# Top-k attention and a rational FFN on one core: planner lengths set anew, weight signs and weight roundings given to GpSimd, steps in another order

## The chip, the cores and the metric

The kernel runs on one core of a Trainium2 chip. The metric is the device time of one execution in microseconds, the median over runs. A core has five instruction queues that run side by side: TensorE (PE), VectorE (DVE), ScalarE (ACT), GpSimd (POOL) and SyncE (SP, which only issues transfers here). Each queue works strictly in its own order, and engines wait for each other through semaphores.

## The reference

Attention over 8 batches of 8 heads, 576 positions, head size 64, where every row keeps only its 32 largest scores; its output, as 4608 tokens of 512 features, goes through a feed-forward layer whose activation is a quotient of polynomials.

```python
scores = (q @ k.T) / sqrt(64)
kth    = 32nd largest of each row
attn   = softmax(where(scores >= kth, scores, -1e9))
x      = (attn @ v)                       # reshaped to 4608 x 512
h      = x @ w_in                         # 512 x 2048
P      = a[0] + a[1]*h + a[2]*h**2 + a[3]*h**3
Q      = 1 + |b[0]|*|h| + |b[1]|*h**2
out    = (P / (Q + 1e-6)) @ w_out         # 2048 x 512
```

The two weight matrices reach the kernel as 64-bit floats.

## The kernel before, in words

The program is written by a planner. `add(engine, length, emit, after, key, ...)` enters a step with the engine or the engines that may run it, an assumed length, what it must follow and a priority. `Plan.run` then plays all steps forward by these lengths: whenever an engine is free, `choose` takes the ready step with the smallest key and calls its `emit`, so the order of the play is the order of the program on each engine. Nothing of this is decided on the chip: lengths and keys move instructions, and the chip's own durations then decide what waits. A table, `KEY`, holds the priorities, which engines a step may use (the first named has it at once, another only after a delay from `ALT`), and how strongly TensorE is kept at one kind of matmul (`STF`, `STR`).

**Weights.** 32 blocks of 128x512 (`w0` to `w31`; 16 of `w_in`, 16 of `w_out`) are rebuilt from 64-bit words in `weight_block`: a load (SP), `sign` (L388 on GpSimd or L391 on ScalarE), `ends` (L394, ScalarE), `merge` (L399, VectorE), `size` (L404, ScalarE, an absolute value), `join` (L412, GpSimd, sign times size), then `high_part`, a rounding to TensorE's short format (`affine`, L283 on ScalarE or L285 on GpSimd) into `win_h` or `wout`, `low_part` (L429, GpSimd, the remainder), and `put` (SP), which stores the remainder to be fetched again later.

**Attention.** A unit is 128 rows of one pair of heads (named batch_pair_tile). Per head: scores `s` on TensorE (L695 in plain 32-bit for batch 0, L699 in the short format later, L690 for tail rows), a copy `sb` on ScalarE (L706), the top-32 search on VectorE (L710 to L764), a bias `st` (L291 and L842 on GpSimd around `junk` L833 and `z` L838 on ScalarE), the exponential `e` (L803, ScalarE), masked products `pr` (L807, VectorE), transposes `trp` (L962, TensorE), copies `p` (L294, ScalarE), and `av` (L986), probabilities times values.

**FFN ("moe").** 18 chunks of 256 tokens, each in 8 groups: `ph` (L1165, 24 matmuls: high times high, low times high, high times low parts), the polynomials on ScalarE and GpSimd, `gg` (a rounding, L283 or L285, and its remainder L1234 on GpSimd), and `po` (L1318, 12 matmuls). `m0_0_3` is group 3 of chunk 0 of batch 0.

Attention of one batch runs beside the FFN of the batch before it; in batch 0 it runs beside the rebuilding of the weights.

Of the kernel before, what the change touches and what calls it, by code (L numbers as in the profile page):

```python
# [36 lines left out]
class Plan:  # L37
# [54 lines left out]
    def run(self):  # L92
# [12 lines left out]
        while left:  # L105
            assert events, "the plan is stuck"
            now = max(now, heapq.heappop(events)[0])
            while ends and ends[0][0] <= now + 1e-9:
                for h in heapq.heappop(ends)[2].give:
                    h.users -= 1  # L110
                    if h.users == 0:
                        self.ring[h.tag][h.slot] = now
                        self.left[h.tag] += 1
            again = True
            while again:
                again = False
                for e in engines:
                    if free[e] > now + 1e-9:
                        continue
                    q = soon[e]  # L120
                    while q and q[0][0] <= now + 1e-9:
                        s = heapq.heappop(q)[2]
                        heapq.heappush(ready[e], (s.key, s.n, s))
                    s = self.choose(e, ready[e], q, now)
                    if s is None:
                        continue
                    for h in s.take:
                        self.grab(h)
# [12 lines left out]
                    heapq.heappush(events, (s.end, s.n))
                    if s.give:
                        back = s.end + (2.2 if e == "SP" else self.BACK)
                        heapq.heappush(ends, (back, s.n, s))
                        heapq.heappush(events, (back, s.n))
                    for d in s.next:
                        lag = max(self.LAG[e][a] + (a != e) * KEY['SLACK'].get(a, 0.0) for a in d.alts)
                        d.ready = max(d.ready, s.end + lag + d.later)
                        d.wait -= 1
                        if not d.wait:  # L150
                            for i, a in enumerate(d.alts):
                                at = d.ready + (KEY['ALT'][a] * d.alt if i else 0.0)
                                heapq.heappush(soon[a], (at, d.n, d))
                                heapq.heappush(events, (at, d.n))
                            heapq.heappush(events, (d.ready, d.n))
        return now

    def choose(self, e, ready, soon, now):
        kept, got = [], None
        closed = set()  # L160
        stay = KEY['STF'] if self.kind == "f" else KEY['STR']
        items = sorted(ready, key=lambda i: (i[0] - stay * self.stays(e, i[2]), i[1]))
        ready.clear()
        for n, item in enumerate(items):
            s = item[2]
# [14 lines left out]
        s = got[2]  # L180
# [10 lines left out]
def tile_topk_attention__then__rational_ffn(  # L191
# [28 lines left out]
    QL = QF // 2  # L220
# [5 lines left out]
    HW = KEY['HW']  # L226
# [10 lines left out]
    def add(*args, **kwargs):  # L237
        return plan.add(*args, **kwargs)
# [434 lines left out]
    def add_tile(t):  # L673
# [255 lines left out]
    def add_values(u):  # L929
# [221 lines left out]
    def add_group(x, o, g, key, split, xs, oholds):  # L1151
# [392 lines left out]
```

## Time and profile before

| | us |
|---|---|
| median of 3 runs (lowest, highest) | 1460.62 (1460.04, 1462.09) |
| the profiled execution, its own time | 1459.78 |
| span of its trace | 1458.0 |
| TensorE busy in the span | 1382.9 (95%) |
| ScalarE / VectorE / GpSimd busy | 1305.3 / 1301.1 / 1126.6 |

The profiled execution took 1.78 us more than its span; that share lies around the first and last instruction. A stretch of time is named by its microseconds from the start of the span ("0 to 205"). Matmuls overlap in TensorE, so their pace is read from the distance of their starts, not from one duration.

### The profile page before, as it was taken

What the parts mean: (1) busy time and instruction counts of PE and PEld (TensorE: products, weight loads), DVE (VectorE), ACT (ScalarE), POOL (GpSimd) and SP (SyncE); (2) the same over time, 40 slices, a digit from 0 to 9 for tenths busy, and PEclk for the clock granted to TensorE, in tenths of its full rate; (3) what the DMA queues carried; (4) which work ended last, traced back from release to release, by engine and by line L of the source; (5) the groups of instructions that cost most, each with busy time, mean ns of one, the idle gap of its engine ahead of it and who ended that gap; (6) DMA issues with size and microseconds to landing.
All of it is one profiled execution on the core that took longest, in us unless ns stands there. A gap on an engine that the chain in (4) does not pass through costs nothing.

```text
span 1458.0 us, 32829 instructions
## 1 busy us (share of the span) xinstructions
PE 1382.9 (95%) x9569; PEld 1155.3 (79%) x9569; DVE 1301.1 (89%) x5826; ACT 1305.3 (90%) x2925; POOL 1126.6 (77%) x1761
## 2 busy tenths in 40 slices
PE   4667899999999999999999999999999999999997
PEld 2435678888888878888888888888888888888995
DVE  7999989999999999999999999999999999996000
ACT  7888899999999998999899999999999999999673
POOL 5786687687867887779688877778777976876995
PEclk9777899999999999999999999999999999999999
DMA  7656766668666867577666777678667766664564
GB/s 249 232 175 210 218 215 201 184 190 248 192 211 183 245 193 226 162 223 225 210 211 202 221 224 213 186 212 224 212 182 215 228 185 216 181 189 145 173 210 118
DMA packets 162687, 296.67 MB, mean 203 GB/s; under 512 B 22976, under 2 KB 73152, under 8 KB 162496
## 3 DMA queue, kind: packets, MB, share of 16 engines
q1 hardware_dynamic: 162496, 294.47, 66.1%
q8 instruction: 78, 1.28, 0.4%
q14 instruction: 113, 0.93, 0.2%
HBM read 229.64 MB, written 18.87 MB: 170 GB/s over the span
## 4 chain that ended last, share of the span: by engine, by line
PE 79%; ACT 7%; DVE 7%; POOL 3%; DMA 2%; issue 1%; SPq 0%; ACTq 0%; POOLq 0%
PE ph_m L1165 22%; PE po_m L1318 21%; PE av L986 9%; PE trp L962 8%; PE s L699 8%; PE ph_t L1165 3%; PE po_t L1318 3%; PE s L690 2%; DVE pr L807 1%; ACT e L803 1%; PE s L695 1%; DVE m L748 1%; PE av L999 1%; ACT sb L706 1%; ACT p L294 1%
## 5 line engine op out<-in xcount | busy, mean ns | idle before, releaser
L1318 PE MATMUL po_m<-wout,gg_m 128*128 128x512 f32 x1024 | 336.9, 410 | 1.7 <-ACT ob_m L294 1.1
L1165 PE MATMUL ph_m<-xh_m,win_h 128*128 128x256 f32 x1024 | 301.7, 295 | 2.9 <-ACT w_w L404 1.7
L1165 PE MATMUL ph_m<-xh_m,wi_m 128*128 128x256 f32 x1024 | 288.4, 282 | 1.0 <-DMA wi_m<-win_l 1.0
L1165 PE MATMUL ph_m<-xl_m,win_h 128*128 128x256 f32 x1024 | 289.1, 282 | 0.0
L748 DVE MAX8 m<-all 128x8 f32<-128x144 f32 (+1 forms) x864 | 266.2, 308 | 4.7
L807 DVE SCALAR_TENSOR_TENSOR pr<-sb,m,e 128x576 f32<-128x576 f32 x288 | 232.2, 807 | 17.5 <-ACT e L803 15.5
L706 ACT COPY sb<-s 128x576 f32<-128x576 f32 x288 | 184.1, 644 | 54.3 <-PE s L699 33.2
L962 PE MATMUL trp<-ident,pr 128*128 128x128 f32 x1312 | 217.5, 282 | 12.9 <-ACT p L294 11.0
L803 ACT ACTIVATE e<-sb,st 128x576 f32<-128x576 f32 x288 | 216.4, 752 | 12.7 <-DVE hi L740 7.2
L294 ACT COPY p<-trp 128x512 f32<-128x512 f32 (+1 forms) x448 | 208.8, 481 | 10.9 <-PE trp L962 10.2
L1165 PEld LDWEIGHTS ph_m<-xh_m,win_h 128*128 128x128 f32 x1024 | 194.1, 190 | 22.4 <-issue 8.8
L1228 POOL TENSOR_TENSOR pa_m<-pa_m,hv_m 128x512 f32<-128x512 f32 x128 | 165.3, 1293 | 59.3 <-ACT hv_m L1225 58.5
L962 PEld LDWEIGHTS trp<-ident,pr 128*128 128x128 f32 x1312 | 162.8, 144 | 53.3 <-ACT p L294 18.5
L1318 PE MATMUL po_m<-wl_m,gg_m 128*128 128x512 f32 x512 | 202.3, 395 | 0.0
L1165 PEld LDWEIGHTS ph_m<-xl_m,win_h 128*128 128x128 f32 x1024 | 194.8, 190 | 2.3
L1165 PEld LDWEIGHTS ph_m<-xh_m,wi_m 128*128 128x128 f32 x1024 | 194.7, 190 | 1.6 <-DMA wi_m<-win_l 1.4
L1318 PEld LDWEIGHTS po_m<-wout,gg_m 128*128 128x128 f32 x1024 | 172.1, 189 | 28.8 <-issue 2.3
L1247 POOL TENSOR_TENSOR pa_m<-pa_m,hv_m 128x512 f32<-128x512 f32 x128 | 165.5, 1293 | 21.8 <-ACT hv_m L283 12.3
L759 DVE MATCH_REPLACE8 all<-m,all 128x144 f32<-128x144 f32 x576 | 168.7, 293 | 0.0
L1234 POOL TENSOR_TENSOR gg_m<-pa_m,gg_m 128x512 fp32r<-128x512 f32 x128 | 165.3, 1293 | 3.3 <-ACT gg_m L283 0.2
L986 PE MATMUL av<-p,vm 128*64 128x256 f32 x1280 | 160.4, 399 | 3.1 <-ACT p L294 3.1
L986 PEld LDWEIGHTS av<-p,vm 128*64 128x64 f32 x1280 | 89.8, 143 | 62.7 <-issue 10.5
(123 smaller groups left out, 3538.9 us busy)
## 6 DMA issues: line engine op xcount, KB each, us to landing
wi_m<-win_l SPq DMA_DIRECT2D x128, 512.0 KB, 4.0
wl_m<-wout_l SPq DMA_DIRECT2D x256, 256.0 KB, 3.3
vm<-in_v_dram SPq DMA_DIRECT2D x96, 320.0 KB, 3.2
q<-qx SPq DMA_DIRECT2D x224, 128.0 KB, 2.8
km<-in_qk_dram SPq DMA_DIRECT2D x32, 352.0 KB, 3.4
w_w<-in_moe_w_in_dram SPq DMA_DIRECT2D x16, 512.0 KB, 5.1
w_w<-in_moe_w_out_dram SPq DMA_DIRECT2D x16, 512.0 KB, 4.8
out_dram<-ob_m SPq DMA_DIRECT2D x64, 128.0 KB, 2.7
```

The source lines that it names most:

```text
L294: (nc.scalar.copy if plan.at == "ACT" else nc.vector.tensor_copy)(out, x)
L706: nc.scalar.copy(t.sb, t.s[:, :, 0:HF])
L748: nc.vector.max(t.m[:, o : o + 8], getattr(t, src))
L759: nc.vector.match_replace(y, t.m[:, o : o + 8], x, NEG)
L803: nc.scalar.activation(t.e, t.sb, AF.Exp, scale=SCALE, bias=t.st)
L807: nc.vector.scalar_tensor_tensor(out=t.pr, in0=t.sb, scalar=t.kth, in1=t.e, op0=ALU.is_ge, op1=ALU.mult, accum_out=u.ss[:, t.h : t.h + 1] ...
L962: nc.tensor.transpose(u.ps[i][:, c * P : (c + 1) * P], u.pr[:, x], ident)
L986: nc.tensor.matmul(pair.av[d, 0 : 2 * P], lhs, x, start=(c == 0), stop=(c == NJ))
L1165: nc.tensor.matmul(y.ph[:, f * NT : (f + 1) * NT], w, z[:, c, :], start=(c == 0 and i == 0), stop=(c == HP - 1 and i == 2),)
L1228: engine().tensor_tensor(out=y.pa, in0=y.pa, in1=y.va, op=ALU.mult)
L1247: nc.gpsimd.tensor_tensor(out=x, in0=x, in1=z, op=ALU.mult)
L1318: nc.tensor.matmul(o.po[i], z, w, start=(ff == 0 and n == 0), stop=(ff == NF - 1 and n == 2),)
```

## The change

The planner's numbers change, and with them which engine runs two kinds of weight steps. In `KEY`, 40 of 72 entries have other numbers and one, `STA`, is new; the table stands on one line in the file, and only the entries with a name or an engine in the text are shown here.

```diff
 KEY = {
...
-       'WH': ('ACT', 'POOL'),
+       'WH': ['POOL', 'ACT'],
...
-       'AV': -3.535776,
+       'AV': 4.132998,
...
-       'SB': ['ACT'],
+       'SB': ['POOL', 'ACT'],
...
-       'STF': 119.319167, 'STR': 12.516198,
+       'STA': 67.169251, 'STF': 30.907148, 'STR': 2.560445,
...
@@ class Plan
     BACK = 0.17
-    CHANGE = 0.085
+    IN, OUT = {"f": 0.0, "r": 0.0, "a": 0.143}, 0.247
@@ Plan.run
-                        if s.kind == "r" != self.kind:
-                            s.length += self.CHANGE
+                        if s.kind != self.kind:
+                            s.length += self.IN[s.kind] + (self.OUT if self.kind == "a" else 0.0)
@@ Plan.choose
-        stay = KEY['STF'] if self.kind == "f" else KEY['STR']
+        stay = KEY[{"f": 'STF', "a": 'STA'}.get(self.kind, 'STR')]
@@ lengths
-    dma = lambda n, words: max(0.52 * n, words * 4 / 260e3)
+    dma = lambda n, words: max(0.52 * n, words * 4 / 295e3)
@@ plain scores
-                    give=[kv.khold, u.pair.q.hold], crit=True, kind="f" if kv.plain else "r")
+                    give=[kv.khold, u.pair.q.hold], crit=True, kind="a" if kv.plain else "r")
@@ av
-                    take=[] if m else [avh] + ([] if u.chunk.parts or u.mixed else [u.chunk.hold]))
+                    take=[] if m else [avh] + ([] if u.chunk.parts or u.mixed else [u.chunk.hold]), kind="a")
@@ polynomials
-            e2 = add("ACT", 0.62, size, [e1], ku + 0.2, give=[mm])
+            e2 = add("ACT", act(512), size, [e1], ku + 0.2, give=[mm])
```

`WH` names the engines of the weights' rounding, `SB` those of the weights' sign. The play now gives 21 of the 32 signs and 29 of the 32 weight roundings to GpSimd; before, ScalarE had all 64. Of other roundings 9 go from GpSimd to ScalarE and 3 the other way. A sign made by GpSimd is one `tensor_scalar` with two operations over every second 32-bit word. VectorE and TensorE keep the same instructions in another order.

GpSimd at the start of the program, from its 13th row, before:

```order
L412 TENSOR_TENSOR w_w0_1_135<-w_w0_0_133,w_w0_1_135 128x512
L291 TENSOR_SCALAR st_0_0_0_166<-m_0_0_0_165 128x2
L429 TENSOR_TENSOR w_w0_0_133<-w_w0_1_135,win_h_80 128x512
L412 TENSOR_TENSOR w_w1_1_138<-w_w1_0_136,w_w1_1_138 128x512
L784 TENSOR_TENSOR fl_0_246<-all_0_0_0_158,m_0_0_0_165 128x2x3
L788 TENSOR_TENSOR fl_0_246<-m_0_0_0_165 128x2
L429 TENSOR_TENSOR w_w1_0_136<-w_w1_1_138,win_h_80 128x512
L842 TENSOR_TENSOR st_0_0_0_166<-st_0_0_0_166,z_0_0_0_209 128x2
```

and of the change:

```order
L388 TENSOR_SCALAR w_w0_1_139<-w_w0_0_137 128x512
L388 TENSOR_SCALAR w_w1_1_147<-w_w1_0_145 128x512
L388 TENSOR_SCALAR w_w2_1_162<-w_w2_0_160 128x512
L412 TENSOR_TENSOR w_w0_1_139<-w_w0_0_137,w_w0_1_139 128x512
L388 TENSOR_SCALAR w_w3_1_180<-w_w3_0_178 128x512
L291 TENSOR_SCALAR st_0_0_0_169<-m_0_0_0_168 128x2
L285 TENSOR_SCALAR win_h_80<-w_w0_1_139 128x512
L412 TENSOR_TENSOR w_w1_1_147<-w_w1_0_145,w_w1_1_147 128x512
L429 TENSOR_TENSOR w_w0_0_137<-w_w0_1_139,win_h_80 128x512
```

Signs (L388) stand ahead of the joins now, and the rounding into `win_h` (L285) stands here between join and remainder (L429); before, GpSimd had only joins and remainders of the weights.

TensorE around the first `po` (group 0 of chunk 0; `s_0_3_2_1` are the scores of batch 0, pair 3, tile 2, second head), before:

```order
L1165 MATMUL ph_m0_0_1_1820<-xh_m0_0_872,wi_m0_0_1_543 128x256
L1318 MATMUL po_m0_0_0_1965<-wout0_81,gg_m0_0_0_1798 128x512 x2
L1318 MATMUL po_m0_0_0_1965<-wl_m0_0_0_0_530,gg_m0_0_0_1798 128x512
L962 MATMUL trp0_0_2_1_1973<-ident_65,pr_0_2_1_1825 128x128 x4
L1318 MATMUL po_m0_0_1_1983<-wout0_81,gg_m0_0_0_1798 128x512 x2
L1318 MATMUL po_m0_0_1_1983<-wl_m0_0_0_0_530,gg_m0_0_0_1798 128x512
L695 MATMUL s_0_3_2_0_1997<-ka_0_2_216,q_0_2_2_1528 128x288 x2
```

and of the change:

```order
L695 MATMUL s_0_3_2_0_1934<-ka_0_2_192,q_0_2_2_1505 128x288 x2
L962 MATMUL trp0_0_2_1_1950<-ident_65,pr_0_2_1_1857 128x128 x4
L962 MATMUL trp1_0_2_1_1960<-ident_65,pr_0_2_1_1857 128x128 x4
L962 MATMUL trp2_0_2_1_1980<-ident_65,pr_0_2_1_1857 128x128
L695 MATMUL s_0_3_2_1_2005<-ka_0_2_192,q_0_2_2_1505 128x288 x2
L1318 MATMUL po_m0_0_0_2018<-wout0_81,gg_m0_0_0_1965 128x512 x2
L1318 MATMUL po_m0_0_0_2018<-wl_m0_0_0_0_472,gg_m0_0_0_1965 128x512
L1165 MATMUL ph_m0_0_1_2032<-xh_m0_0_885,win_h_80 128x256
L1165 MATMUL ph_m0_0_1_2032<-xl_m0_0_886,win_h_80 128x256
```

The first `po` stood ahead of the scores `s_0_3_2_0` and `s_0_3_2_1`; it now stands behind both. Ahead of it stood the 48 `ph` of two groups before, and stand the 24 `ph` of one now.

TensorE ahead of `av_0_3_3`, the last full block of batch 0, before:

```order
L1165 MATMUL ph_m0_0_5_2624<-xh_m0_0_872,win_h_80 128x256
L1165 MATMUL ph_m0_0_5_2624<-xl_m0_0_873,win_h_80 128x256
L1165 MATMUL ph_m0_0_5_2624<-xh_m0_0_872,wi_m0_0_5_2496 128x256
L1318 MATMUL po_m0_0_1_1983<-wout5_86,gg_m0_0_2_2461 128x512 x2
L1318 MATMUL po_m0_0_1_1983<-wl_m0_0_2_1_2035,gg_m0_0_2_2461 128x512
L962 MATMUL trp1_0_3_3_2711<-ident_65,pr_0_3_3_2583 128x128 x4
L690 MATMUL s_1_4_3_0_2722<-km_1_3_2657 128x288 x2
L699 MATMUL s_1_0_0_0_2732<-ka_1_0_1537,q_1_0_0_2090 128x288 x4
L962 MATMUL trp2_0_3_3_2743<-ident_65,pr_0_3_3_2583 128x128
L1318 MATMUL po_m0_0_0_1965<-wout6_87,gg_m0_0_3_2671 128x512 x2
L1318 MATMUL po_m0_0_0_1965<-wl_m0_0_3_0_2482,gg_m0_0_3_2671 128x512
L986 MATMUL av_0_3_3_2757<-p0_0_2_3_2537,vm_0_3_2_2166 64x256
```

and of the change:

```order
L1165 MATMUL ph_m0_0_4_2545<-xl_m0_0_886,win_h_80 128x256
L1165 MATMUL ph_m0_0_4_2545<-xh_m0_0_885,wi_m0_0_4_2381 128x256
L1318 MATMUL po_m0_0_0_2018<-wout3_84,gg_m0_0_1_2304 128x512 x2
L1318 MATMUL po_m0_0_0_2018<-wl_m0_0_1_1_639,gg_m0_0_1_2304 128x512
L962 MATMUL trp1_0_3_3_2635<-ident_65,pr_0_3_3_2510 128x128 x4
L1318 MATMUL po_m0_0_1_2098<-wout3_84,gg_m0_0_1_2304 128x512 x2
L1318 MATMUL po_m0_0_1_2098<-wl_m0_0_1_1_639,gg_m0_0_1_2304 128x512
L1318 MATMUL po_m0_0_0_2018<-wout4_85,gg_m0_0_2_2499 128x512 x2
L1318 MATMUL po_m0_0_0_2018<-wl_m0_0_2_0_2196,gg_m0_0_2_2499 128x512
L962 MATMUL trp2_0_3_3_2669<-ident_65,pr_0_3_3_2510 128x128
L690 MATMUL s_1_4_3_0_2671<-km_1_3_2598 128x288 x2
L986 MATMUL av_0_3_3_2682<-p0_0_2_3_2477,vm_0_3_2_2245 64x256
```

Before, `ph` of group 5 and `po` of group 3 stand ahead of that `av`; now it is `ph` up to group 4 and `po` up to half of group 2. Counted over the whole program ahead of it, 144 `ph` and 39 `po` became 120 `ph` and 27 `po`.

## Rows read from the trace of the kernel before

**Rows 1.** Page, busy time of the engines, and the group of `pr`.

```profile
PE 1382.9 (95%) x9569; PEld 1155.3 (79%) x9569; DVE 1301.1 (89%) x5826; ACT 1305.3 (90%) x2925; POOL 1126.6 (77%) x1761
...
L807 DVE SCALAR_TENSOR_TENSOR pr<-sb,m,e 128x576 f32<-128x576 f32 x288 | 232.2, 807 | 17.5 <-ACT e L803 15.5
```

**Rows 2.** Busy time by stretch: PE, PEld, DVE, ACT, POOL, granted clock, DMA, GB/s.

```profile
0.00:205.00 205.00, 145.89 (x659) 94.42 (x660) 185.09 (x782) 171.15 (x386) 145.37 (x260) 0.82 0.68 215
205.00:1350.00 1145.00, 1139.06 (x8305) 973.67 (x8304) 1115.55 (x5043) 1067.44 (x2430) 891.00 (x1414) 1.00 0.68 205
1350.00:1458.00 108.00, 97.94 (x610) 87.22 (x608) 0.42 (x2) 66.69 (x110) 90.20 (x89) 0.97 0.53 167
```

**Rows 3.** Waits of DVE, 0 to 225: total, times, longest us.

```profile
DVE s L724 <- ACT sb L706: 10.3, 7, 7.0
DVE pr L807 <- ACT e L803: 8.5, 13, 1.1
```

**Rows 4.** Waits of PE, 0 to 210.

```profile
PE s L695 <- DVE pr L807: 19.6, 10, 4.4
```

**Rows 5.** ScalarE, groups, 0 to 205: busy us, mean ns, idle before.

```profile
L391 ACT ACTIVATE w_w<-w_w 128x512 f32<-128x512 f32 x32 | 21.6, 675 | 1.6 <-DMA w_w<-in_moe_w_out_dram 1.0 <-DMA w_w<-in_moe_w_in_dram 0.6
...
L283 ACT ACTIVATE win_h<-w_w 128x512 fp32r<-128x512 f32 x16 | 10.1, 632 | 0.4 <-POOL w_w L412 0.3
```

**Rows 6.** Waits of POOL, 0 to 210.

```profile
POOL w_w L412 <- ACT w_w L404: 24.0, 8, 11.1
POOL w_w L429 <- ACT win_h L283: 7.7, 7, 2.2
POOL w_w L429 <- ACT wout L283: 7.7, 5, 3.1
POOL st L842 <- ACT z L838: 4.4, 5, 1.9
```

**Rows 7.** POOL, the group of biases, 0 to 205.

```profile
L842 POOL TENSOR_TENSOR st<-st,z 128x2 f32<-128x2 f32 (+1 forms) x20 | 3.9, 196 | 4.5 <-ACT z L838 4.4
```

**Rows 8.** ScalarE, timeline at 74 and 128 us: start, duration.

```profile
74.05 0.62 ACT L283 ACTIVATE wout<-w_w 128x512 fp32r<-128x512 f32 x1
128.16 0.63 ACT L283 ACTIVATE wout<-w_w 128x512 fp32r<-128x512 f32 x1
```

**Rows 9.** DVE, timeline: a wait for `e`, at 76 us.

```profile
76.06 0.81 DVE L807 SCALAR_TENSOR_TENSOR pr<-sb,m,e 128x576 f32<-128x576 f32 x1 [0.51 <-ACT e L803]
```

**Rows 10.** DVE, timeline: a wait for `e`, at 129 us.

```profile
129.65 0.82 DVE L807 SCALAR_TENSOR_TENSOR pr<-sb,m,e 128x576 f32<-128x576 f32 x1 [0.62 <-ACT e L803]
```

**Rows 11.** POOL, groups by shape over the whole span.

```profile
L1234 POOL TENSOR_TENSOR gg_m<-pa_m,gg_m 128x512 fp32r<-128x512 f32 x128 | 165.3, 1293 | 3.3 <-ACT gg_m L283 0.2
L285 POOL TENSOR_SCALAR gg_m<-pa_m 128x512 fp32r<-128x512 f32 x126 | 78.2, 621 | 5.0 <-PE po_m L1318 2.7
```

**Rows 12.** TensorE, timeline at 420 us.

```profile
420.11 0.28 PE L1165 MATMUL ph_m<-xh_m,win_h 128*128 128x256 f32 x1
420.23 0.28 PE L1165 MATMUL ph_m<-xl_m,win_h 128*128 128x256 f32 x1
```

**Rows 13.** TensorE, timeline at 1447 us, the last `po`.

```profile
1446.97 0.63 PE L1318 MATMUL po_m<-wout,gg_m 128*128 128x512 f32 x2
1447.44 0.40 PE L1318 MATMUL po_m<-wl_m,gg_m 128*128 128x512 f32 x1
```

**Rows 14.** TensorE, timeline at 216 us, `av_0_3_3`.

```profile
216.46 2.38 PE L986 MATMUL av<-p,vm 128*64 128x256 f32 x20 [0.25 <-ACT p L294]
```

**Rows 15.** DVE, timeline at 208 us, second `pr` of that pair.

```profile
207.76 0.80 DVE L807 SCALAR_TENSOR_TENSOR pr<-sb,m,e 128x576 f32<-128x576 f32 x1
```

**Rows 16.** POOL, timeline at 148 us, the first `gg`.

```profile
148.50 0.63 POOL L285 TENSOR_SCALAR gg_m<-pa_m 128x512 fp32r<-128x512 f32 x1
```

**Rows 17.** Chain that ended last, 0 to 205, shares by line.

```profile
by line: PE s L695 10.1%; PE av L986 7.2%; issue 6.5%; PE trp L962 5.3%; POOL cf L460 5.0%; ACT e L803 4.6%; PE ph_m L1165 4.2%; DVE pr L807 3.9%; ACT p L294 3.8%; ACT sb L706 3.5%; POOL w_w L429 3.3%; ACT w_w_b L394 3.3%; POOL w_w L412 3.3
```

More of the change, by code (lines that the diff above doesn't have):

```diff
@@ L19 @@
 PSUM = bass.MemoryType.PSUM
-KEY = {'OB': 16, 'K0': -0.28899, 'W0': 8.051968, 'STAY': 0.0, 'WH': ('ACT', 'POOL'), 'XH': ('POOL', 'ACT'), 'TH': 0, 'EU': 3.317342, 'SC': 0, 'HW': 256, 'Q0': ('POOL', 'ACT'), 'Q1': ('POOL',), 'SPLIT': (0, 1, 2, 3, 4, 5, 6, 7), 'XS': 1, 'P1': ('ACT', 'POOL'), 'P3': ('ACT', 'POOL'), 'RH': ('POOL', 'ACT'), 'p2': ('POOL', 'DVE'), 'p4': ('POOL',), 'ratio': ('POOL', 'DVE'), 'ratio_low': ('POOL',), 'URG': -236.940941, 'PT': 3.624573, 'AV': -3.535776, 'MOE': 250.353405, 'QT': 12.339559, 'KT': -1024.739554, 'EL': 1.0, 'LOOK': 13.192386, 'T': 5.289204, 'KL': -3.109586, 'KH': -8.857491, 'PJ': 408607.619053, 'WL': 3.813792, 'EX': 1.354535, 'EW': 32506.804284, 'ALT': {'ACT': 7.648546, 'DVE': 418.393903, 'POOL': 38.077554}, 'WG': 4.626767, 'QL': -3.100556, 'QH': -0.899155, 'PACE': 9.594453, 'B4': 0, 'RT': 1.0, 'DA': 9.729067, 'PU': (2, 2, 2, 2), 'SB': ['ACT'], 'SU': 0, 'JD': (), 'WK': -0.07211, 'PM': -5.222566, 'WI': 0, 'WO': 0, 'MS': 1.367923, 'NM': ('POOL', 'ACT'), 'WD': ('ACT',), 'LP': ('POOL',), 'FL': ('DVE',), 'VL': 548.608015, 'RI': -11.942583, 'ROOM': {'s': 2, 'mm': 2, 'o': 2, 'k': 4, 'kr': 1, 'km': 1, 'q': 2, 'qr': 1, 'v': 2, 'sb': 5, 'lo': 2, 'hi': 2, 'pr': 2, 'p0': 1, 'p1': 1, 'p2': 1, 'm': 4, 'u': 4, 'fl': 2, 'x': 2, 'xm': 1, 'xs': 1, 't': 4, 'ob': 3, 'wi': 2, 'wl': 4, 'tt': 5}, 'TN': 2, 'IL': 13.292096, 'SLACK': {'DVE': 0.0, 'PE': 0.0, 'ACT': 0.0, 'POOL': 0.0}, 'CF': 83.339795, 'LD': 0.761693, 'CL': 0.0, 'C0': 11.274467, 'ML': 1.392146, 'GL': 1.395418, 'STF': 119.319167, 'STR': 12.516198, 'SIZE': {'tt': 4096}}
@@ new lines @@
+KEY = {'OB': 16, 'K0': 13.303452, 'W0': 24.665155, 'STAY': 0.0, 'WH': ['POOL', 'ACT'], 'XH': ('POOL', 'ACT'), 'TH': 0, 'EU': -6.33561, 'SC': 0, 'HW': 256, 'Q0': ('POOL', 'ACT'), 'Q1': ('POOL',), 'SPLIT': (0, 1, 2, 3, 4, 5, 6, 7), 'XS': 1, 'P1': ('ACT', 'POOL'), 'P3': ('ACT', 'POOL'), 'RH': ('POOL', 'ACT'), 'p2': ('POOL', 'DVE'), 'p4': ('POOL',), 'ratio': ('POOL', 'DVE'), 'ratio_low': ('POOL',), 'URG': -130.582522, 'PT': -0.867947, 'AV': 4.132998, 'MOE': 65.519289, 'QT': 2.481227, 'KT': -5.785962, 'EL': 1.0, 'LOOK': 9.292689, 'T': 4.599216, 'KL': -22.168793, 'KH': 0.120246, 'PJ': 283356.121515, 'WL': 0.038413, 'EX': -8.145565, 'EW': 8862.816374, 'ALT': {'ACT': 2.797506, 'DVE': 300.280479, 'POOL': 25.426874}, 'WG': 4.452997, 'QL': -16.24214, 'QH': 11.99219, 'PACE': 10.855309, 'B4': 0, 'RT': 1.0, 'DA': 1.471092, 'PU': [2, 2, 2, 2], 'SB': ['POOL', 'ACT'], 'SU': 0, 'JD': (), 'WK': -4.152913, 'PM': -0.275068, 'WI': 0, 'WO': 0, 'MS': 1.775628, 'NM': ('POOL', 'ACT'), 'WD': ('ACT',), 'LP': ('POOL',), 'FL': ('DVE',), 'VL': 686.2294, 'RI': 8.713432, 'ROOM': {'s': 2, 'mm': 2, 'o': 2, 'k': 4, 'kr': 1, 'km': 1, 'q': 2, 'qr': 1, 'v': 2, 'sb': 5, 'lo': 2, 'hi': 2, 'pr': 2, 'p0': 1, 'p1': 1, 'p2': 1, 'm': 4, 'u': 4, 'fl': 2, 'x': 2, 'xm': 1, 'xs': 1, 't': 4, 'ob': 3, 'wi': 2, 'wl': 4, 'tt': 5}, 'TN': 2, 'IL': 15.884027, 'SLACK': {'DVE': 0.0, 'PE': 0.0, 'ACT': 0.0, 'POOL': 0.0}, 'CF': -13.594874, 'LD': 1.48874, 'CL': 2.277205, 'C0': 13.817918, 'ML': 0.0, 'GL': 3.959851, 'STA': 67.169251, 'STF': 30.907148, 'STR': 2.560445, 'SIZE': {'tt': 4096}}
```

## Prediction, made before the result

> **What bounds the kernel now.** I read the page's busy line first: TensorE is busy 95% of the span [rows 1]. A share of the whole hides where the other 5% lies, so the next view is busy time by stretch [rows 2]. From 205 to 1350 us TensorE works 1139.06 of 1145 us, so 5.9 are idle; from 1350 to the end it is idle 10.1; from 0 to 205 it is idle 59.1. Of 75.1 idle us, 59.1 lie in the start. The granted clock there is 0.82, that is between the two levels, while it is 1.00 in the middle. Only work that ends the start sooner, or puts more FFN work into it, can shorten the kernel by more than a few us.
>
> What bounds the start? VectorE is busy 185.09 of 205 us there, ScalarE 171.15, GpSimd 145.37 [rows 2]. TensorE waits for `pr` of VectorE 19.6 us before plain scores [rows 4]. So VectorE carries the start, and what delays VectorE delays all: 10.3 us for `sb`, of which one wait of 7.0 is the first score of the kernel, and 8.5 us for `e`, 13 waits [rows 3]. Without that first one, 10.3 - 7.0 + 8.5 = 11.8 us are waits on ScalarE that its queue can cause. GpSimd waits 24.0 us for ScalarE's `size`, and 7.7 + 7.7 = 15.4 for ScalarE's weight roundings [rows 6]. The chain of the start says the same: it runs through many hands, with 3.3% of 205 us each in GpSimd's remainders and joins of the weights, together 13.5 us [rows 17].
>
> **The change, part by part.**
>
> *Signs and roundings leave ScalarE.* 21 signs at 0.675 and 29 roundings at 0.632 [rows 5] are 14.2 + 18.3 = 32.5 us of ScalarE's 171.15 in the start, 19%. (Other roundings, 9 to ScalarE and 3 away, are spread over the run.) What is it worth? Such a rounding stands just ahead of the softmax chain in two cases: at 74.05 one of 0.62 us, and VectorE waits 0.51 at 76.06; at 128.16 one of 0.63, and VectorE waits 0.62 at 129.65 [rows 8 to 10]. These 1.1 us go for sure; of the other 10.7 I give 19%, the moved share of the queue, 2.0: a lower estimate of 3.1. The upper estimate takes ScalarE as a queue in which waiting goes with busy over free time: 171.15/33.85 = 5.1 before, 138.65/66.35 = 2.1 after, so 59% of 11.8 fall, 7.0. A ScalarE step that comes sooner brings forward the whole chain behind it, not only the next step, so I go nearer to the upper one: **-5.6**. The ends are 0 (the steps left on ScalarE wait for something else) and -11.8.
>
> *The same steps come to GpSimd.* A rounding costs 0.621 there [rows 11]. A sign on GpSimd is not in the trace. Its nearest row is that one-input rounding, 0.621; the dearest comparable row is a two-input step, 1.293 [rows 11]. It has one input, so I take 0.65, with both ends kept. 29 x 0.621 + 21 x 0.65 = 31.7 us; GpSimd has 205 - 145.37 = 59.6 idle in the start, so it would be at 86%. This costs nothing while the idle time covers it, and much of that idle time is waits that now vanish: the remainder (L429) no longer waits for ScalarE's rounding (15.4), and `size` comes sooner from a shorter queue (part of the 24.0). Without that cover the 31.7 us would stand in the weights' chain. The weights feed `ph`, then `gg`. The first `gg` starts at 148.50 [rows 16]; in the new order GpSimd has 18 signs, 24 roundings, 3 joins and 3 remainders more ahead of it, 18 x 0.65 + 24 x 0.621 + 6 x 1.293 = 34.4 us. Less 15.4 that is 19 us later, less all of the 24.0 it is 5 us sooner. What is queued behind each on GpSimd are 20 biases (L842) in the start [rows 7], and `e` on ScalarE, then `pr` on VectorE wait for them. Now GpSimd waits 4.4 us for ScalarE's `z` before a bias [rows 6], so it is GpSimd that is early. I cost this at 0 and keep the loss for the rivals.
>
> [...]
>
> *The new order of TensorE and VectorE.* The first `po` moves behind `s_0_3_2_1`, so the scores on which VectorE waits come first. Ahead of `av_0_3_3`, where batch 0 ends, there are now 24 `ph` and 12 `po` fewer. At full clock starts of `ph` lie 0.12 us apart [rows 12], and two `po` take 0.47 [rows 13]: 24 x 0.12 + 12 x 0.235 = 5.7 us of FFN work less done by then. It has to be done later, where TensorE is full, so it is a loss unless that `av` comes sooner. Before the change it starts at 216.46, 8.7 us after its last `pr` at 207.76 [rows 14, 15]. Of VectorE's rows, 6 fewer (some 1.4 us) stand ahead of that `pr`; with 5.7 us less in TensorE's own queue the `av` can come sooner by 1.4 to 5.7. I take the middle, 3.6, and the term is **+2.1**, with ends 0 and +4.3.
>
> *Middle and end.* From 205 to 1350 TensorE is idle only 5.9 us [rows 2]; the new kinds and stay times only reorder there, and the work is the same: 0, with ends -5.9 (all waits gone) and +6 (as many again). Behind the last `av` of batch 7 there are 24 `ph` and 15 `po` fewer than before; TensorE is full until 1447 us, so work only changes places. The last `po` begins at 1447.44 [rows 13] and copies and the last transfer follow as now: 0. The new lengths for transfers and absolute values have no cost but through the order.
>
> **Sum.** -5.6 + 2.1 = -3.5, against the profiled execution's 1459.78 (span 1458.0 and 1.78 around it) 1456.3. That execution is 0.84 under the median of the runs shown, 1460.62; against the median the sum gives **1457.1**. Its own range is 1452 to 1461. A time within 0.2% (2.9 us) of before is about what can't be told from no change.
>
> **The rivals.**
>
> *All waits for ScalarE go.* The `e` and `sb` waits vanish and the order costs nothing: 1460.6 - 11.8 = 1448.8. For it: the longest wait for `e` is 1.1 us [rows 3], so a small advance removes each whole. Against: a freed VectorE meets the next limit soon, its own 185 busy us of 205 [rows 2].
>
> *The biases eat the gain.* GpSimd at 86% delays the biases by as much as ScalarE gained: 1460.6 + 2.1 = 1462.7. For it: all joins and remainders are 1.29 us long [rows 11] and a bias of 0.196 [rows 7] sits behind one. Against: GpSimd waits 4.4 us before biases now [rows 6].
>
> *Slower: GpSimd becomes the bound of the start.* Each of 20 biases [rows 7] waits half a step of 1.29, 12.9 us, of which half is covered: 6.4. If that comes with the gain of 5.6 gone and the order's 2.1 lost, it gives 1460.6 + 2.1 + 5.3 = 1468, where 5.3 is also near 38% (31.7 us on 64 joins and remainders of 1.29, 82.6 us) of the 13.5 us that these already have in the chain [rows 17]. It decides from the point at which new waits of `e` for biases pass 3.5 us (the gain gone); from 6.4 the kernel is measurably slower.
>
> *Signs at the dear end.* At 1.293 a sign, 21 x 0.64 = 13.5 us more stand on GpSimd, 94% busy in the start; if half of it reaches the chain, 1457.1 + 6.7 = 1463.8. For it: a comparison and a subtraction over strided words, unlike a rounding. Against: one input, as the rounding at 0.621 [rows 11]. [...]
>
> **How the numbers follow.** Forecast 0.47 (0.31 of it faster by more than 0.2%, 0.14 within, 0.02 slower); all waits gone 0.12; biases eat the gain 0.13 (0.11 within, 0.02 slower); GpSimd bound 0.20; dear signs 0.08 (half within, half slower). Faster 0.43, within 0.29, slower 0.28. From 1447 to 1467 the forecast, the first and second rival, the dear signs, and the near part of the GpSimd case are held; left out are the far side of that case (0.1) and a gain beyond all waits, or a middle that changes by more than its ends (0.08).
>
> **What would show each step right or wrong.** Right: in the start ScalarE some 32 us less busy and GpSimd some 32 more; the waits of `pr` for `e` and of the fold for `sb` down from 11.8 to about 6; no wait of GpSimd's remainders on ScalarE; a sign near 0.65; waits of `e` for L842 still about 2 us; `av_0_3_3` at 211 to 215 us; TensorE's idle time from 205 to 1350 still near 6. Wrong: `e` waiting for L842 by more than 3.5 us; a sign over 0.9; VectorE's idle time in the start unchanged although ScalarE is less busy, which would say that TensorE's or VectorE's own order sets the start; or a middle whose idle time moves by several us, which would say that the new order's value lies there and not in the start.

## The result, and the profile after

The changed kernel is slower: 1476.28 us in the median of 6 runs, 1460.68 for the kernel before, a ratio (of the means of the runs, here and below) of 1.011 with a 95% interval of [1.009, 1.0131]. Of the 15.6 us between the medians the prediction had -3.5; the time lies above its range.

The busy line of the page after answers to [rows 1]; the second row is the group of `pr` in the whole span.

```profile
PE 1387.7 (94%) x9569; PEld 1161.5 (79%) x9569; DVE 1303.3 (88%) x5826; ACT 1284.5 (87%) x2880; POOL 1184.0 (80%) x1806
...
L807 DVE SCALAR_TENSOR_TENSOR pr<-sb,m,e 128x576 f32<-128x576 f32 x288 | 232.8, 808 | 34.6 <-ACT e L803 31.4
```


TensorE has the same work (1387.7 against 1382.9 us) but VectorE's `pr` waits 31.4 us for `e` where it waited 15.5. Busy time by stretch, in the columns of [rows 2], says where:

```profile
0.00:205.00 205.00, 136.68 (x567) 84.92 (x568) 172.53 (x735) 137.75 (x314) 191.36 (x293) 0.77 0.62 199
205.00:1350.00 1145.00, 1134.94 (x8262) 975.12 (x8264) 1115.76 (x5027) 1061.50 (x2415) 893.28 (x1413) 1.00 0.69 206
1350.00:1476.00 126.00, 116.04 (x745) 101.44 (x741) 14.98 (x66) 85.28 (x154) 99.33 (x102) 0.97 0.51 162
```


It is the start. There ScalarE is 33.4 us less busy (171.15 to 137.75; 32.5 were forecast), but GpSimd 46.0 us more (145.37 to 191.36; 31.7 were forecast), and VectorE and TensorE both do less (172.53 for 185.09, 136.68 for 145.89). The middle changes less: TensorE idle 10.1 us for 5.9, and a part of that still lies in batch 0, which now ends later. What filled GpSimd is in its groups from 0 to 205 us:

```profile
L388 POOL TENSOR_SCALAR w_w<-w_w 128x512 f32<-128x512 f32 x21 | 41.1, 1962 | 7.7 <-DMA w_w<-in_moe_w_in_dram 7.7
...
L285 POOL TENSOR_SCALAR wout<-w_w 128x512 fp32r<-128x512 f32 x15 | 9.4, 629 | 0.1
L285 POOL TENSOR_SCALAR win_h<-w_w 128x512 fp32r<-128x512 f32 x15 | 9.3, 623 | 0.2
```


The 30 roundings (one more than the text ahead of the prediction counts) cost 0.62 to 0.63, as the row of before had it. A sign costs 1.962 us: 41.1 us for 21, three times the 0.66 of the planner and over the dearest row that I had allowed, 1.293.

Who waits for it? First VectorE, 0 to 225 us, as in [rows 3], then ScalarE, 0 to 205:

```profile
DVE pr L807 <- ACT e L803: 21.7, 21, 3.0
DVE s L724 <- ACT sb L706: 12.3, 6, 7.0
```

```profile
ACT junk L833 <- POOL st L291: 14.2, 9, 3.6
...
ACT e L803 <- POOL st L842: 4.6, 3, 3.0
```


Waits of `pr` for `e` rose from 8.5 to 21.7. ScalarE, which was to be relieved, now waits 14.2 + 4.6 = 18.8 us for GpSimd's two small steps of the softmax bias, `st` (L291 and L842). Before it was 2.4, and GpSimd waited 4.4 us for ScalarE's `z` instead [rows 6]; ScalarE's rows of before, 0 to 205:

```profile
ACT e L803 <- POOL st L842: 2.0, 3, 1.4
ACT junk L833 <- POOL st L291: 0.4, 1, 0.4
```


GpSimd in turn waits for little after its first load (0 to 210, as in [rows 6]):

```profile
POOL w_w L388 <- DMA w_w<-in_moe_w_in_dram: 7.7, 1, 7.7
POOL st L291 <- DVE m L748: 2.5, 2, 1.7
```


The waits of 24.0, 7.7 and 7.7 us of [rows 6] are gone, as forecast, and not idle time but signs took their place. The chain of the start has moved onto GpSimd: joins, remainders, signs and roundings of weights are 53% of it, against 6.6% in [rows 17].

```profile
by line: POOL w_w L412 16.3%; POOL w_w L429 15.4%; POOL w_w L388 14.3%; issue 8.2%; POOL cf L460 8.0%; POOL win_h L285 3.7%; POOL wout L285 3.4%; DMA w_w<-in_moe_w_in_dram 2.9%; POOL kl L572 2.0%; PE av L986 2.0%; DVE pr L807 2.0%; PE s L69
```


One such case, from the timelines of GpSimd, ScalarE and VectorE around 50 us (start, duration, work, idle time before):

```profile
48.98 1.95 POOL L388 TENSOR_SCALAR w_w<-w_w 128x512 f32<-128x512 f32 x1
50.90 1.26 POOL L429 TENSOR_TENSOR w_w<-w_w,wout 128x512 fp32r<-128x512 f32 x1
52.14 0.19 POOL L291 TENSOR_SCALAR st<-m 128x2 f32<-128x2 f32 x1
```

```profile
52.36 0.32 ACT L833 ACTIVATE junk<-m,st 128x32 f32<-128x32 f32 x1 [2.35 <-POOL st L291]
...
52.68 0.73 ACT L803 ACTIVATE e<-sb,st 128x576 f32<-128x576 f32 x1
```

```profile
53.44 0.81 DVE L807 SCALAR_TENSOR_TENSOR pr<-sb,m,e 128x576 f32<-128x576 f32 x1 [2.99 <-ACT e L803]
```


A sign and a remainder stand ahead of a bias step of 0.19 us. VectorE's last step on `m` ahead of it (L748) had ended at 49.58 us, but the bias began only at 52.14, as the remainder ended (50.90 and 1.26). ScalarE idles 2.35 us for that step, its `junk` and `e` run late, and VectorE, on whose `pr` TensorE's plain scores wait 31.2 us from 0 to 210 (19.6 before [rows 4]), idles 2.99 us. By the planner's 0.66 the sign would have ended 1.3 us sooner.

Where the time goes can be summed at the end of batch 0. `av_0_3_3` started at 216.46 [rows 14]; now:

```profile
228.89 2.38 PE L986 MATMUL av<-p,vm 128*64 128x256 f32 x20
```


That is 12.4 us later, with 5.7 us less FFN work done ahead of it: 18.1 us lost there. The spans differ by 18.0 (1476.0 and 1458.0); nothing of note is lost or won behind it.

The granted clock of the start fell as well, from 0.82 to 0.77 in the mean. Its two levels show in the trace of before: 0.50 from 57 to 73 us, 1.00 from 74 to 80. One matmul of the plain scores took 632 ns from 0 to 205 in the mean, where it took 572 before. TensorE idles 68.3 us there, where it idled 59.1; how much of the 12.4 us goes through its clock is not separated by any run.

### The profile page after: what moved, and what is told of

Read it like the earlier page. It is cut to its first block, busy times and chain, and to the rows that moved or that the text cites. A ratio compares the mean times of both kernels' runs of the same rounds, so it can differ in the third digit from the quotient of the medians.

```text
span 1476.0 us, 32852 instructions
## 1 busy us (share of the span) xinstructions
PE 1387.7 (94%) x9569; PEld 1161.5 (79%) x9569; DVE 1303.3 (88%) x5826; ACT 1284.5 (87%) x2880; POOL 1184.0 (80%) x1806
## 4 chain that ended last, share of the span: by engine, by line
PE 72%; POOL 12%; DVE 6%; ACT 4%; DMA 2%; issue 2%; SPq 1%; POOLq 0%; ACTq 0%
PE ph_m L1165 22%; PE po_m L1318 20%; PE trp L962 7%; PE av L986 7%; PE s L699 7%; PE po_t L1318 3%; PE ph_t L1165 2%; POOL w_w L412 2%; POOL w_w L429 2%; POOL w_w L388 2%; PE s L690 2%; DVE m L748 1%; DVE pr L807 1%; PE av L999 1%; POOL cf L460 1%
## 5 line engine op out<-in xcount | busy, mean ns | idle before, releaser
L748 DVE MAX8 m<-all 128x8 f32<-128x144 f32 (+1 forms) x864 | 267.5, 310 | 4.3
L807 DVE SCALAR_TENSOR_TENSOR pr<-sb,m,e 128x576 f32<-128x576 f32 x288 | 232.8, 808 | 34.6 <-ACT e L803 31.4
L962 PEld LDWEIGHTS trp<-ident,pr 128*128 128x128 f32 x1312 | 163.3, 145 | 54.3 <-ACT p L294 13.6
L1247 POOL TENSOR_TENSOR pa_m<-pa_m,hv_m 128x512 f32<-128x512 f32 x128 | 165.4, 1292 | 23.7 <-ACT hv_m L283 10.8
```

Of the source, the lines that this page charges most:

```text
L748: nc.vector.max(t.m[:, o : o + 8], getattr(t, src))
L807: nc.vector.scalar_tensor_tensor(out=t.pr, in0=t.sb, scalar=t.kth, in1=t.e, op0=ALU.is_ge, op1=ALU.mult, accum_out=u.ss[:, t.h : t.h + 1] ...
L962: nc.tensor.transpose(u.ps[i][:, c * P : (c + 1) * P], u.pr[:, x], ident)
```

## The experiments

Three theories were set against each other. The first: the sign on GpSimd is dear, and what queues behind it on GpSimd is late. The second: the 30 roundings there are what delays the biases. The third: the new order of TensorE and VectorE costs of itself. "Order held" means that the planner plays as in the kernel named, and only the engine that a step is issued on, or its instruction, changes, at the same place of the program; the order of TensorE, VectorE and SyncE stays, row for row.

| run | median us | ratio to before, 95% interval | GpSimd busy 0 to 205 | `st` waits of ScalarE | `e` waits of `pr` | `av_0_3_3` starts |
|---|---|---|---|---|---|---|
| before (profile) | 1459.78 | | 145.4 | 2.4 | 8.5 | 216.5 |
| the change | 1476.28 | 1.0110 [1.0090, 1.0131] | 191.4 | 18.8 | 21.7 | 228.9 |
| signs back | 1465.38 | 1.0037 [1.0022, 1.0053] | 156.8 | 0.2 | 13.3 | 218.7 |
| roundings back | 1472.09 | 1.0095 [1.0069, 1.0120] | 177.1 | 5.9 | 17.6 | 221.6 |
| both back | 1469.68 | 1.0074 [1.0047, 1.0100] | 138.0 | 0 | 19.0 | 220.9 |
| cheap sign | 1461.20 | 1.0012 [0.9997, 1.0027] | 173.0 | 2.3 | 9.3 | 214.1 |
| before + dear signs | 1478.90 | 1.0134 [1.0108, 1.0160] | 168.0 | 17.5 | 22.6 | 236.7 |
| before + cheap signs | 1464.75 | 1.0035 [1.0023, 1.0048] | 156.6 | 7.4 | 9.3 | 219.1 |
| before + roundings | 1461.83 | 1.0015 [1.0001, 1.0029] | 163.1 | 8.2 | 8.6 | 215.8 |
| true sign length | 1467.40 | 1.0053 [1.0032, 1.0075] | 187.7 | 3.4 | 7.2 | 209.6 |

The waits are the sums of ScalarE's waits for GpSimd's `st` from 0 to 205 us and of VectorE's `pr` for `e` from 0 to 225, in each profiled execution. One execution can lie some us from the median of its run: that of "signs back" took 1469.65, that of "true sign length" 1462.95. Each group of runs had its own runs of the kernel before, with medians from 1458.75 to 1460.78, so the ratios are what is compared.

Where an order is held, the time goes roughly with the waits of `pr` for `e`: 8.6 to 9.3 us in the three runs within 0.35% of before, 13.3 at 0.37%, 17.6 to 22.6 in the four from 0.74 to 1.34%. It does not go with the `st` waits alone: with the roundings on ScalarE in this order, `e` is late although ScalarE waits only 0 to 5.9 us for GpSimd's `st`.

### The signs, the roundings and both issued back on ScalarE

```diff
-                if plan.at == "POOL":          # sign, in the first and the third
+                if False:
...
-            affine(hi, o.w, 1.0, 0.0)          # high_part, in the second and the third
+            nc.scalar.activation(hi, o.w, AF.Identity, scale=1.0, bias=0.0)
```

Signs back. 

> The changed kernel with its whole order held, but the 21 signs that it gives to GpSimd are issued on ScalarE at the same places of the program (the output is the same). Theory 1 (the dear sign: 1.962 us each, 41.1 us that fill GpSimd in the start): GpSimd's busy time in the start falls from 191 to about 150 us, the waits of pr for e from 21.7 to under 12 us, and the time from 1476 to 1456 to 1463. Theory 2 (the 30 roundings on GpSimd are what delays the biases): at most a third of the loss goes, 1470 to 1474. Theory 3 (the new order of VectorE and TensorE is what costs): unchanged, 1474 to 1478.

Roundings back. 

> The changed kernel with its order held, the 30 weight roundings that it gives to GpSimd issued on ScalarE at the same places; the 21 signs stay on GpSimd. Theory 1: GpSimd loses 18.7 us of 191 but keeps the 41.1 of the signs, and the remainders wait for ScalarE again: a third to a half of the loss goes, 1468 to 1473. Theory 2: all of it goes, 1458 to 1463. Theory 3: unchanged, 1474 to 1478.

Both back. 

> The changed kernel with its order held, signs and weight roundings all issued on ScalarE as before: what is left is the new order alone. Theory 1 and theory 2: near the kernel before, 1456 to 1464. Theory 3: still slow, over 1470. If it is slower than the run with the signs alone back, the roundings on GpSimd are a gain.

Signs back gave 1465.38: two thirds of the loss is gone (ratio 1.0110 to 1.0037), GpSimd falls to 156.8 and ScalarE's waits for `st` to 0.2. That is the first theory, though 1465.38 lies above its interval, and `pr` still waits 13.3 us for `e`. The roundings back take away little, 1472.09, which lies in the interval of the first theory and speaks against the second; by the ratios it is a seventh of the loss (1.0110 to 1.0095), less than the third to a half that the first theory named, and not clear of noise. Both back gave 1469.68, where the first two theories expected 1456 to 1464: the order by itself, with the engines of before, is 0.74% (10.8 us) slower than the order of before. In it `pr` waits for `e` again, though ScalarE has no wait for `st`:

```profile
DVE pr L807 <- ACT e L803: 19.0, 20, 2.1
```


So a part for the third theory was left open here: does this order cost of itself, or only when the steps that it was planned to have on GpSimd stand on ScalarE? The four runs also show that the kinds do not add up. With the roundings on ScalarE the dear signs on GpSimd change little (1.0074 to 1.0095, intervals that overlap); with the roundings on GpSimd they change much (1.0037 to 1.0110).

### Signs on GpSimd in the order of before

```diff
-                if plan.at == "POOL":
+                if number not in (4, 6, 9, 12, 14, 15, 16, 20, 21, 23, 24):
```

> The kernel before with its order held, the signs of the same 21 blocks issued on GpSimd at the places where ScalarE had them. Theory 1: 41 us go onto a GpSimd that is idle 59.6 us in the start, a good part of it in waits for these same blocks: 1465 to 1475. Theory 2 and theory 3: within 4 us of before, 1457 to 1464.

1478.9 us, above even the first theory's interval. The move alone, without the new table, kinds or lengths, costs 1.34%, as much as the whole change (the intervals overlap). ScalarE's waits show the same two rows as after the change, and `av_0_3_3` comes 20.2 us later at the same work, as the span does (1478.2 to 1458.0):

```profile
ACT junk L833 <- POOL st L291: 11.2, 8, 2.2
...
ACT e L803 <- POOL st L842: 6.3, 5, 3.0
```

```profile
236.68 1.52 PE L986 MATMUL av<-p,vm 128*64 128x256 f32 x12 [0.25 <-ACT p L294]
```


Here GpSimd is busy 168 of 205 us, not full. It is no question of capacity alone: 21 signs of 1.96 us, placed among the joins and biases of the order of before, were enough.

### What makes the sign dear

```python
for i in range(16): nc.gpsimd.tensor_scalar(y, odd, 0.0, 0.5, op0=ALU.is_ge, op1=ALU.subtract)    # L213; L215 on dense rows
for i in range(16): nc.gpsimd.tensor_scalar(y, odd, 1.0, 0.0, op0=ALU.mult, op1=ALU.add)          # L217; L219 on dense rows
for i in range(16): nc.gpsimd.tensor_scalar(y, odd, 0.0, None, op0=ALU.is_ge)                     # L221; L223 on dense rows
for i in range(16): nc.gpsimd.tensor_scalar(y, odd, 1.0, -1.0, op0=ALU.min, op1=ALU.max)          # L225
for i in range(16): nc.gpsimd.tensor_scalar(y, odd, 0.5, 0.5, op0=ALU.mult, op1=ALU.subtract)     # L227
for i in range(16): nc.gpsimd.tensor_tensor(out=y, in0=odd, in1=row, op=ALU.mult)                 # L229
for i in range(16): nc.scalar.activation(y, odd, AF.Sign)                                         # L231, ScalarE
```

> Nothing of the reference is computed: 16 instructions in a row of each of nine forms on GpSimd (128x512), and 16 signs on ScalarE, by themselves. If the comparison makes the sign dear (1.96 us), the comparison over a dense row costs near 1.9 too, and multiply-add over every second word near 0.62. If the step of 8 bytes makes it dear, every form over every second word costs over 1.2 and the dense comparison near 0.62. If other engines slowed it in the kernel, the comparison over every second word takes well under 1.9 here.

GpSimd's groups of this run; `raw` is every second word, `row` a dense row:

```profile
L227 POOL TENSOR_SCALAR y<-raw 128x512 f32<-128x512 f32 x16 | 31.1, 1943 | 1.3
L213 POOL TENSOR_SCALAR y<-raw 128x512 f32<-128x512 f32 x16 | 31.1, 1941 | 2.1 <-DVE raw L206 0.9
L215 POOL TENSOR_SCALAR y<-row 128x512 f32<-128x512 f32 x16 | 30.7, 1921 | 1.3
L221 POOL TENSOR_SCALAR y<-raw 128x512 f32<-128x512 f32 x16 | 24.1, 1507 | 1.3
L223 POOL TENSOR_SCALAR y<-row 128x512 f32<-128x512 f32 x16 | 23.8, 1487 | 1.3
L229 POOL TENSOR_TENSOR y<-raw,row 128x512 f32<-128x512 f32 x16 | 20.6, 1288 | 1.3
L217 POOL TENSOR_SCALAR y<-raw 128x512 f32<-128x512 f32 x16 | 10.2, 637 | 1.3
L225 POOL TENSOR_SCALAR y<-raw 128x512 f32<-128x512 f32 x16 | 10.1, 633 | 1.3
L219 POOL TENSOR_SCALAR y<-row 128x512 f32<-128x512 f32 x16 | 9.9, 617 | 1.3
```


The price goes with the form: of the three readings the first holds, and it was too narrow. In this run the comparison alone takes 1.49 to 1.51 us, with the subtraction 1.92 to 1.94; a multiplication with a subtraction costs 1.94 too, without any comparison. The constants differ between these forms as well, which these runs do not separate; in the kernel before, a multiplication and an addition of a value that comes from a column (L1246, 128x512) takes 0.70, far from 1.94. Multiplication with addition takes 0.62 to 0.64, minimum with maximum 0.63. The step of 8 bytes adds 0.02 in each of the three pairs (L213 and L215, L217 and L219, L221 and L223). And 1.94 alone against 1.96 in the kernel: beside the other engines the sign took 0.02 us more. So my reading "one input, as the rounding" had the wrong thing in view; the two rows between which I put the price (0.621 and 1.293) do not enclose it.

### A cheap sign in the same order

Clamping to ±2^-60 gives the sign, times 2^-60, in the cheap form, as long as the words are larger than that in size; the size is multiplied by 2^60 in its own step, so the product is unchanged.

```diff
-                    nc.gpsimd.tensor_scalar(o.w, o.raw[1].bitcast(F32), 0.0, 0.5, op0=ALU.is_ge, op1=ALU.subtract)
-                    o.size = 2.0
+                    nc.gpsimd.tensor_scalar(o.w, o.raw[1].bitcast(F32), 2.0**-60, -(2.0**-60), op0=ALU.min, op1=ALU.max)
+                    o.size = 2.0**60
```

> The changed kernel with its order held on all five engines and the sign on GpSimd made by clamping between -2^-60 and 2^-60 (minimum, then maximum; 0.633 us alone), with the size multiplied by 2^60: the output is the same. It gives the order the sign length for which it was planned. If the dear sign is the whole cause, the start costs no more than before: 1455 to 1461. If the order of VectorE and TensorE costs of itself, as the 1469.7 with both kinds back on ScalarE suggests, it stays at 1464 to 1470. If GpSimd is too full even so, the biases still wait: over 1470.

1461.2 us, ratio 1.0012 [0.9997, 1.0027]: not to be told from the kernel before, and 0.2 us above the first theory's interval. All five engines have the order of the change, row for row, and one instruction is 1.3 us shorter, 21 times. Of the change's 1.10% this takes away 0.98. The first `gg`, at 148.50 before [rows 16], comes at 177.82 after the change and at 162.59 here: the weights on GpSimd were late as well, not the biases alone. GpSimd's sign, VectorE's waits for ScalarE, and `av_0_3_3`:

```profile
L388 POOL TENSOR_SCALAR w_w<-w_w 128x512 f32<-128x512 f32 x21 | 13.6, 650 | 10.9 <-DMA w_w<-in_moe_w_in_dram 9.5
```

```profile
DVE s L724 <- ACT sb L706: 11.2, 7, 7.0
DVE pr L807 <- ACT e L803: 9.3, 17, 1.1
```

```profile
214.15 2.38 PE L986 MATMUL av<-p,vm 128*64 128x256 f32 x20
```


This settles the open part: the order costs 10.8 us with both kinds on ScalarE, but no more than 0.27%, the upper end of the interval, with both on GpSimd and the signs at the length for which it was planned. It also shows what the gain that I forecast comes to; the next section takes that up.

> The kernel before with its order held and the same 21 signs on GpSimd in the cheap form. With the dear form this move cost 19 us (1478.9). If the price of the instruction is the cause and not the move, it is within 4 us of before: 1457 to 1464; if any sign on GpSimd delays its joins and biases, over 1466.

The same form in the order of before gave 1464.75, 0.35% [0.23, 0.48] slower, where the dear one was 1.34% slower. It lies 0.75 us above the interval for the price alone and under the 1466 of the other. The price is most of it; a rest is the move: ScalarE waits 7.4 us for `st` here, against 2.4.

### Roundings on GpSimd in the order of before

```diff
-            affine(hi, o.w, 1.0, 0.0)
+            (nc.scalar.activation(hi, o.w, AF.Identity, scale=1.0, bias=0.0) if number in (11, 22) else
+             nc.gpsimd.tensor_scalar(hi, o.w, 1.0, 0.0, op0=ALU.mult, op1=ALU.add))
```

> The kernel before with its order held, 30 of 32 weight roundings issued on GpSimd at their places. In the changed order the same move was worth 4.3 us (1469.7 with both kinds on ScalarE, 1465.4 with the roundings on GpSimd). If that is the roundings' own worth (ScalarE's queue shorter by 19 us, remainders that don't wait for it): 1454 to 1457. If it was worth something only in an order planned for it: 1458 to 1462. If GpSimd is too full for them: over 1462.

1461.83, ratio 1.0015 [1.0001, 1.0029]: nothing won, as the second interval had it. ScalarE is 11.7 us less busy in the start (171.15 to 159.46), and `pr` waits 8.6 us for `e`, as before (8.5).

### Plans with other numbers

```diff
-       'SB': ['POOL', 'ACT'],          # first and second run
+       'SB': ['ACT'],
...
-    dma = lambda n, words: max(0.52 * n, words * 4 / 295e3)     # second run
+    dma = lambda n, words: max(0.52 * n, words * 4 / 260e3)
...
-            s1 = add({e: {"ACT": 0.68, "POOL": 0.66}[e] ...     # third run
+            s1 = add({e: {"ACT": 0.68, "POOL": 1.96}[e] ...
...
-       'STA': 67.169251, 'STF': 30.907148, 'STR': 2.560445,           # fourth run: the whole table of before
+       'STA': 119.319167, 'STF': 119.319167, 'STR': 12.516198,
```

> The changed kernel planned anew with the signs allowed on ScalarE alone; every other number of the change stays. If the 5.7 us that are left with the signs issued back are there because that order was planned for signs of 0.66 us on GpSimd, an order planned without them gives 1454 to 1461. If the new keys, kinds and transfer lengths cost of themselves, it stays at 1463 to 1470.

> As the run before it, with the planner's length of a transfer at the old 260e3. With the signs back, ScalarE waits 6 to 9 us for weight loads in the start, against 1.6 before. If the shorter assumed transfers put ScalarE's steps too early, this gives 3 us or more less than the run with 295e3, and those waits near 2 us; if not, the two are within 3 us.

> The changed kernel planned anew with 1.96 us, as measured, in place of 0.66 for a sign on GpSimd; 19 signs still go there, and they still take 1.96. If the work itself is too much for GpSimd, it stays at 1472 to 1479; if the wrong length misplaced the steps around it, 1460 to 1468.

> The new kinds, lengths of transfers and absolute values with the old table (the new entry for the third kind set to the old 119.3): the part of the change that is not the table. Signs and roundings are on ScalarE as before. If the lengths and kinds cost of themselves, over 1465; if only the table and its engines do, 1456 to 1464.

The true length in the plan: 1467.4, half of the loss gone, in the interval for misplaced steps. 19 signs still cost 1.97 on GpSimd, which is busy 187.7 us of 205, hardly less than after the change; yet ScalarE waits only 3.4 us for `st`. `av_0_3_3` comes at 209.59, with 96 `ph` and 24 `po` ahead of it: 9.3 us less FFN work than before and 6.9 us sooner, so 2.4 us lost there, where the change lost 18.1. So a GpSimd nearly as full did not hold up the start in this plan, which knows the price. How much of the loss is due to place and how much to the work can't be read from this run, since the whole order is another.

Signs on ScalarE alone, planned anew, was a miss: 1473.44 (1.0090), above both intervals. With the old transfer length it is 1470.17 (1.0064), 3.3 us less, where 3 or more was asked; but the intervals of the two still touch, ScalarE's waits for weight loads fall only from 6.5 to 3.7 us and not to 2, and TensorE idles more in the middle, so I count nothing as shown on transfers. In both `av_0_3_3` comes early (207.2 and 207.9): 9.2 and 8.5 us sooner than before, with only 6.1 and 2.9 us less FFN work ahead of it. So the start is mended, but TensorE idles 13.7 and 18.8 us from 205 to 1350 against 5.9. The old table with the new kinds and lengths: 1487.08 (1.0191), in the interval in which they cost of themselves, with the old table; again much of it is in the middle, 22.8 us idle. Each plan's middle differs, in many small waits that I did not take apart. That a table fits the lengths that it was found with is my reading, not shown; what one number of it is worth can't be read from such runs. The middle of the last run, in the columns of [rows 2]:

```profile
205.00:1350.00 1145.00, 1122.19 (x8149) 958.36 (x8149) 1113.90 (x5005) 1048.22 (x2389) 876.76 (x1398) 1.00 0.67 203
```


## Why the prediction was wrong, point by point

**What bounds the kernel:** right. The start decides; the change's whole loss is there by `av_0_3_3` (18.1 of 18.0 us of span). From it to the end TensorE idles 17.0 us, against 15.5 before; the middle and the end were costed at 0.

**"Its nearest row is that one-input rounding, 0.621; the dearest comparable row is a two-input step, 1.293 ... I take 0.65":** this step failed. It measured 1.962 us, 21 of them 41.1 us where I had 13.7. The number of inputs does not tell the price: by themselves, one-input forms took 0.62 to 1.94 us and the two-input product 1.29. The price went with the form, and no row of before with 128x512 words had a comparison or a subtraction of a constant. The dearest row at hand should not have been trusted as an upper bound.

**"I cost this at 0 and keep the loss for the rivals":** it failed with the price. Idle time in the start fell from 59.6 us to 13.6, and the biases waited behind the signs. The 4.4 us that GpSimd waited for `z` [rows 6] stood ahead of L842 alone. Most of the new wait is one step earlier, at L291 (14.2 us); ahead of that step GpSimd had waited only 2.6 us in the start, a wait that the working leaves out. The sign of being wrong that I named, `e` waiting for L842 by more than 3.5 us, came too (4.6).

**The slower rivals.** "GpSimd becomes the bound of the start" named this mechanism: `pr` has 13.2 us of new waits for `e` (8.5 to 21.7), twice the 6.4 from which it called the kernel measurably slower. Its 1468 was too low by 8; it let a bias wait behind steps of 1.29 us, not of 1.96, and its sum has 5.3 where the line before it gives 6.4, without a reason. "Signs at the dear end" had the cause at too low a price: the surplus is 27.6 us, not 13.5 (with which GpSimd would have been 93% busy, not 94%), and with half of that on the chain, as it assumed, it would have come to 1470.9. From the cheap sign to the dear one 15.1 us were measured, about half; that share was a guess with no row behind it, so its fitting is luck.

**-5.6 for ScalarE's shorter queue:** not borne out, as seen where the sign is cheap. ScalarE is busy 148.07 instead of 171.15 us in the start there, yet VectorE waits 9.3 for `e` and 11.2 for `sb`, against 8.5 and 10.3 [rows 3]. With the roundings alone moved in the order of before the waits for `e` stay (8.6). Waiting did not go with ScalarE's share of busy time, so neither the 7.0 from the queue nor the 1.1 from the two rows came back. Only in the new order is the relief worth something: 0.74% slower with both kinds on ScalarE, 0.12% with both on GpSimd and cheap.

**+2.1 for the order:** the size fits only as part of a sum. With the cheap sign `av_0_3_3` starts at 214.15, 2.3 us sooner (1.4 to 5.7 were allowed) with 5.7 us less done: 3.4 lost, within the 0 to 4.3; by the two spans 2.8. But that is order and relief together, and with the engines of before the order alone costs 10.8 us. I priced the two terms apart, and each depends on the other.

**The sum with the price that I assumed** can be held against the cheap sign, 0.65 us in the kernel. The forecast was 3.5 us faster; measured was 0.12% [-0.03, 0.27] slower, -0.4 to 3.9 us. So the gain was not there either. The dear sign adds the rest, 1.0012 to 1.0110.

## What to carry to other kernels

A step that is moved to another engine has to be priced there in its own form, operation by operation: on GpSimd one-input forms over the same 128x512 words took from 0.62 to 1.94 us. If no row has that form, its upper end is open, and sixteen of them in a row on the chip are a cheap experiment. A step that is long for its queue can cost time ahead of a small one on which a softmax waits, even where the engine is idle a fifth of the time: here 21 signs of 1.96 us on a GpSimd that was idle 37.0 of 205 us brought `av_0_3_3` 20.2 us later in the order of before, about half of their 41. And a plan that knows the true price can lose less: with 1.96 in it half of the loss was gone (ratio 1.0110 to 1.0053) and ScalarE's waits for `st` fell from 18.8 to 3.4 us, though GpSimd was busy 187.7 us of 205 for 191.4.

## What the runs showed of the hardware

On GpSimd, 128x512 words of 32 bits in one `tensor_scalar`, sixteen in a row by themselves: multiply and add 0.617 us over dense rows and 0.637 over every second word, minimum and maximum 0.633, a comparison alone 1.487 and 1.507, comparison and subtraction 1.921 and 1.941, multiply and subtraction 1.943; a two-input product took 1.288, less than a one-input comparison. The step of 8 bytes added 0.020 us in each of these three pairs. The sign by comparison and subtraction took 1.962 in the changed kernel, the one by minimum and maximum 0.650 in the same order. The sign on ScalarE took 0.658 by itself, 0.675 in the kernel before.
